# DeltaNet and MLP-mixer: exchanged chunks for odd head pairs in two of four batch elements

## The chip, the cores and the metric

The kernel runs on one core of a Trainium2 chip. The metric is the device time of one execution in microseconds (us); lower is better. Engines are named as in the profile: PE is TensorE (PEld its weight loads), DVE is VectorE, ACT is ScalarE, POOL is GpSimd, SP is SyncE, which issues all loads and stores here.

## The reference

Two blocks follow each other. The first is a DeltaNet recurrence, for 4 batch elements, 8 heads, 768 tokens and a head dimension of 48; the second a mixer over tokens and channels on rows of 8 x 48 = 384.

```python
k_n = k / (np.linalg.norm(k, axis=-1, keepdims=True) + 1e-06)
for t in range(S):
    y[:, :, t] = einsum('bhd,bhde->bhe', q[:, :, t], state)
    v_old = einsum('bhde,bhd->bhe', state, kt)
    state = state + bt * einsum('bhd,bhe->bhde', kt, vt - v_old)
x = y as (B, S, H * D)
h = np.maximum(x^T @ w_tok1, 0) @ w_tok2      # over tokens, 768 -> 256 -> 768
u = x + h^T
out = u + np.maximum(u @ w_ch1, 0) @ w_ch2    # over channels, 384 -> 1536 -> 384
```

All data are float32, and so are the matmuls.

## The kernel before

**The recurrence in chunks.** The tokens of an element are cut into 12 chunks of 64 (C); two chunks make a unit of 128 tokens (U). There are 24 units u (6 for each element, `b, c = divmod(u, NCH)`) and 48 steps t, one for each chunk of 64 tokens with all 8 heads. Heads stand in 4 pairs p, with a parity i in each. A unit is prepared apart from the state: `prep(u)` (from line 430) takes norms of the keys, turns keys and queries so that features lie along partitions (`kqts`), and makes the masked products p_g (L501, masked in L507); `invert` (L637, L642) and `join` (L715 to L734) invert the triangular matrices. `load_kq` and `load_v` fetch keys, queries and values from DRAM; `stacked` (lines 397 to 404) loads keys (kst) or values (v_st) with four DMA issues, so that of each head pair one head's chunk lies in partitions 0 to 63 and the other's in 64 to 127. Which one depends on the chunk alone: rows `PAR[i ^ cc]`, with cc the chunk in the unit.

**A step**, `recur(t)` (lines 740 to 811), then does the part that needs the state, s0, which lies with its 48 features on partitions 0 to 47 (parity 0) and 64 to 111 (parity 1):

- p_k = keys times state (L757, 8 products), then rest = p_k - v_st on DVE (L762);
- p_y = queries times state (L775) and p_w = inverse times rest (L779), interleaved; w_t is p_w copied by ACT (L783);
- p_s = keys times w_t (L791) and a second sum into p_y (L792), interleaved; the new state s1 = s0 - p_s on DVE (L801);
- two copies of p_y into the rows xb of the element, on ACT (L806).

The first chunk of an element has no p_k and no L775, and the last one no p_s. Each `yield` in it ends a part. A product of 64 rows by 64 columns uses one of the four 64x64 quarters of the PE array; its rows follow from the partitions of its operands and its columns from the partitions of its output. An fp32 product shows as two matmul records. p_k goes from rows of parity i to partitions `PAR[i ^ cc]`: for one step these are two of the four quarters. p_y and p_w together use all four, and so do p_s and the second p_y.

**PSUM** has eight banks: two for prep, three for the mixer, two that p_k, p_y, p_w and p_s take in turn (`ps_seq`), and one for warm-up matmuls (`p_warm`).

**The mixer**, `mixer(b)` (from line 943), takes an element when its 12 steps are written: over tokens (L950, L963), then over channels. Element 0 multiplies plainly (L1030); elements 1 to 3 use 15 combined weight blocks (`wide_fast`, p_r, L922, added up by DVE in L934 and ACT in L931 and L938), whose operands DVE forms in L891. The product with w_ch2 is p_o (L1052), added in L981.

**What sets the order.** Nothing is scheduled by the compiler: `tc.manual_schedule()` keeps every engine's instructions in the order in which they are recorded. All work is in generators, called jobs: k, p, h, f, j, v for a unit's loads and preparation, i for inversions, r for steps, m for mixers, w for weight pieces. A string written out by hand (`order`) tells which job goes on next, each time to its next `yield`; `r24*2 m1` records two parts of step 24 and one of mixer 1. The first half of the string is latency bound (loads and rounding of weights, the first units), the second mixes steps with mixer work.

Of the kernel before, what the change touches and what calls it, by code (L numbers as in the profile page):

```python
# [23 lines left out]
def kernel(  # L24
# [72 lines left out]

    def ps_seq(shape, name):
        return psum.tile(shape, FP32, name=name, tag="seq", bufs=2)
# [119 lines left out]
    p_warm = psum.tile([128, 4, 128], FP32, name="p_warm", tag="warm", bufs=1)  # L219

    def keep_warm(m):

        zero = warm[:, 0:128]
        while True:
            nc.tensor.matmul(
                p_warm[:, 0:m], zero, zero[:, None, :].to_broadcast([128, m, 128])
            )
            yield

    def warm_tiles():  # L230

        while True:
            for j in range(2):
                for r in PAR:
                    nc.tensor.matmul(p_warm[r, j], warm[r, 0:C], warm[r, 0:128])
            yield

    def load_beta():


        rows = mlp_pool.tile([B * H, S], FP32, name="b_rows", tag="xb")
        nc.sync.dma_start(out=rows, in_=beta.rearrange("b h s -> (b h) s"))
        yield
        p_b = ps_prep([128, NQ, B * NP], "p_b")
        for c in range(NQ):
            for par in range(2):
                nc.tensor.matmul(
                    p_b[PAR[par ^ c % 2], c], rows[:, c * C : (c + 1) * C],
                    ident[: B * H, par : B * H : 2],
                )  # L250
# [146 lines left out]
    def stacked(dst, src, u):  # L397
        rows = heads_of(src, u)
        for par in range(2):
            for cc in range(2):  # L400
                nc.sync.dma_start(
                    out=dst[PAR[par ^ cc], :, cc], in_=rows[par, cc]
                )
                yield
# [25 lines left out]
    def prep(u):  # L430
# [6 lines left out]
        bet = beta_st[:, b, :, 2 * c : 2 * c + 2]  # L437
# [15 lines left out]
        nc.vector.tensor_tensor(  # L453
            out=cs, in0=ksum.rearrange("s (p c) -> s p c", c=2), in1=bet, op=ALU.mult
        )
# [41 lines left out]
        for p in range(NP):  # L497
            for cc in range(2):
                for i in range(2):
                    f = PAR[i] if u < TU else FEATS[i]  # L500
                    nc.tensor.matmul(  # L501
                        p_g[cc][PAR[i ^ cc], p], kqt[f, p, cc, 0], kqt[f, p, cc]
                    )
        yield
        for cc in range(2):
            assert cc == 0 or before_in(u) is None or before_in(u) in walked
# [233 lines left out]
    def recur(t):  # L740
# [10 lines left out]
        heads = [(p, i, PAR[i ^ cc], PAR[1 - i]) for p in range(NP) for i in range(2)]  # L751

        if c > 0:
            p_k = ps_seq([128, NP, D], "p_k")
            for p, i, r, _ in heads:
                f = FEATS[i]
                nc.tensor.matmul(p_k[r, p], kqt[f, p, cc, 0], s0[f, p])  # L757
# [4 lines left out]
            nc.vector.tensor_tensor(  # L762
                out=rest, in0=p_k, in1=vsts[u][:, :, cc], op=ALU.subtract
            )
            yield
        else:
            rest = vsts[u][:, :, cc]

        assert u in scaled and u in joined
        p_y = ps_seq([128, NP, D], "p_y")  # L770
        p_w = ps_seq([128, NP, D], "p_w")
        for p, i, r, o in heads:
            if c > 0:
                f = FEATS[i]
                nc.tensor.matmul(  # L775
                    p_y[o, p], kqt[f, p, cc, 1], s0[f, p],
                    start=(p == 0), stop=False,
                )
            nc.tensor.matmul(p_w[r, p], gm[r, 2 * p + cc, TC], rest[r, p])  # L779
# [7 lines left out]
        if on:  # L787
            p_s = ps_seq([128, NP, D], "p_s")
        for p, i, r, o in heads:
            if on:  # L790
                nc.tensor.matmul(p_s[PAR[i], p], gm[r, 2 * p + cc, 0:C], w_t[r, p])  # L791
            nc.tensor.matmul(  # L792
                p_y[o, p], gm[r, 2 * p + cc, GC], w_t[r, p],
                start=(c == 0 and p == 0), stop=(p == NP - 1),
            )
        if cc == 1:
            walked.add(u)
        yield
        if on:
            if c > 0:  # L800
                nc.vector.tensor_tensor(out=s1, in0=s0, in1=p_s, op=ALU.subtract)  # L801
            else:
                nc.vector.tensor_copy(out=s1, in_=p_s)
            yield
        for i in range(2):
            nc.scalar.mul(  # L806
                y[:, :, D * i : D * i + D], p_y[PAR[1 - i]], 1.0 if c else -1.0
            )
# [340 lines left out]
    r12 s m0 v7 r12 w25 r12 w23 p10*3 f9 r12 j8 r13 w23 p12 w23 j8 m0 p11 r13*3 p11*2  # L1149
    w23 x w32 f9 v8 w30 w20 r13*2 k13 w32 w20 p10 r13 p11*3 w20 k13 r14*2 p12 k13 w32  # L1150
    p12 k13*3 m0*2 k13 w30 m0 k13 p11 w30*2 v8 k13 r14 k13*2 r14 p12*2 p11 k13 p12 p13
    r14 p12*3 m0 p12 p13 r14*2 m0 p13 w23 w25 p13 w33 v8*2 m0 j9 r15 p13 m0 w23 p13 r15
    w25 m0 p11 m0 r15 p13 r15 w33 m0*2 r15 p13*2 k14 w33 r15 k14 p13*2 w33 r16 m0 r15
    v8 k14*4 p12 w33 p11 r16 w27 w33 w31 m0 w27 w33 w29 w31*2 p13*2 j9 m0 p13*2 m0 j9
    k14 r16 j9 r16*3 k14 p14*2 r16 m0 r17*2 p14*3 m0*2 r17 i3 r17 i3*4 v10 m0 v10 r17*3
    i3*3 k15 m0 i3*2 v9 r18 i3*2 p14 m0 v10 k14 m0 i3 v9 i3 k15*4 v9 k15*3 m0*2 k14
    i3*9 k14 i3 k14 i3 p14 v9*2 m0*3 k15 r18 k15 p14 i3*6 m0*2 i3 v10 j9 k15 m0*4 k15
    m0*9 r18 p14*2 f11 r18*4 f10*2 p15*2 f12 v10 f12 f11 m0*2 p15*2 f10*2 f13 m0 r19
    p15 f12 f11 m0 f11 m0 r19 p14 f13 j10 f13 m0*2 r19 p15 j10 j11 r19*2 k16*8 m0*2 r19
    j10 j11 v11*3 r20 m0*2 r20 r19 j12 j11 r20 p15 k16 r20 m0 r20*2 p16*2 p15*3 k16 v11  # L1160
    p16*2 r21 r20 r21 m0 p15 r21 p16 r21 j12 p14 j12 k16*2 p14*2 k17*2 r21*3 m0 s k17*5
    p16*2 r22 v11 m0 r22*3 p16 m0 k17*4 r22 s v12 s j13 s p16 r22 k17 p16 r22 r23 p16*3
    v12 r23 v12 p15*4 p17*3 p14 p17 m0 p17 r23 m0 p17*2 r23 m0*2 p16 r23 p17*3 v12 p16
    m0 p17*4 m0 s m0 s*3 p17 m0 f12 m0 j13 s*4 r23 m0*3 v12 m0 i4*5 m0 i4*2 k18*8 m0 i4
    j13 r24 m0 i4 m0*2 r24 f13 r24 k18 m0 i4*2 k18 i4 m0*2 p18 i4 k18 p18*2 m0*2 i4 r24
    i4*3 m0 i4*2 k18 p18 r25 p18 m1 v14 r24 v14*3 i4 r25 m1*2 i4 k19 i4 k19*2 m1*3 r25
    k19 i4*2 v13 j13 r25 i4 p18 r25*2 i4 k19*4 m1 i4*2 m1 r25 v13*2 i4*2 v13 i4 j13 i4
    p19 r26 m1*2 p18 k19*4 m1 v13 r26 p19 m1*5 p18 f14 r26 f14 r26 p18 r26 f15 m1 r26
    m1*3 r26 m1*2 p19 f14 r27*2 f14 m1 r27 f15 p19 f15*2 p19 k20*5 p18 j14 m1*2 p18 p19
    r27*2 j14 j15 m1*2 j14 r27 m1 r27 k20*2 s j15 r28 p18 j15 p19 v14 k20*4 r28 m1*3  # L1170
    k20 m1 v15*2 s*2 p19 v15*2 r28*2 p19 r28 v15 m1 f16*3 r28 r29 p19 p20*2 r28 r29
    p20*2 p19 p20 k21*4 m1*3 p19 k21*4 r29*2 p20 p18*2 p20 m1*3 f17*2 m1*3 r29*3 j16
    m1*2 f17 m1 k21*4 m1*5 r30 j16 m1 r30 p20 m1 p19 m1 p18 m1 j16 p21 r30 p21 p20
    p19*2 p20 r30*3 p20 p21 p20 r31 p20*2 p21 r30 m1 r31*2 v16 r31 v16 m1 p21 f16 k22
    p21*2 r31 p21*2 r31*2 p20 r32 m1 p21*3 m1*2 p21*3 v16*2 i5 m1*2 k22*11 m1*7 v16 j17
    r32 m1*2 j17 f17 i5*2 m1*3 j17 i5 r32 i5*2 p22 r32 v17*2 i5*2 v17 m1*3 i5 m1*2
    r32*2 m1*3 i5*2 r33 r32 v17 r33 j17 v20 m1 i5 v20 i5 r33 p22*2 m1*4 i5 p22*4 m1*10
    r33 j17 v17 m1*3 i5 m1*2 k23*8 m1*3 r33 p22 r33 m1*7 r34*2 p23 m1*7 r33 i5 m1*2 r34
    p22 r34 p22 r34*2 m1 v20 i5*2 m1 r34 i5*2 m1 k23 m1 i5*3 m1*4 k23 r35 p22*2 m1*2
    p22*2 m1 i5*2 k23 m1 p23 m1*4 i5 m1 i5 m1 i5 p23 k23 r35 m1 i5*3 m1*8 v18 v20 i5  # L1180
    f21 p23 v18 f18*2 f19 m1 v18 p23*2 r35*2 m1*5 f18*2 p23*2 m1*3 v18 m1*4 p23 f21
    r35*2 f19 m1*2 f20 p23*4 v20 j18 m1 f19 m1*3 j18 m1*3 j18 j19*2 p23 j19 m1*2 p23
    f21 p22 f21 i6*2 v18 f20*2 r36*2 i6*3 f20 m1 r36 m1 r36 m1 r37*2 i6 m2*5 r36 r37*2
    m2 i6*6 r37 j20 i6*2 v19*2 r37 i6 f19 i6 j20 j21 r38 m2 v19*3 r38 j20 m2 r37 i6 r38
    i6*3 j21 r38*3 m2 r38 m2*2 i6 m2 r39*2 i6 m2*6 v21 r39 m2 r39 m2*2 r39 m2*2 r39
    m2*2 r39 j21 v21*2 m2 r40 m2*2 i6 r40*3 i6 j21 i6 j21 i6*2 r40*3 m2*3 r41 m2 r41 i6
    v21 i6 m2 r41 i6*3 f22*3 f23 m2 r41 v22 m2*6 r41*2 m2*4 v21 m2*5 r41 m2 r42*2 j22
    v22*3 m2*5 f23 r42 j22 f23 j23 r42*2 m2*2 r42*2 m2*7 r43 m2*5 r43*2 m2*3 f22 m2*2
    v23 m2*2 j22 m2*11 r43 m2*3 r43*3 j23*2 r44 m2*3 v23 v22 r44*3 m2*9 r44*3 f23 m2*2
    r45 j23 r45*2 m2 r45 m2*8 r45 m2*14 v23*2 m2*4 r45 r46 j23 m2*5 v23 m2 r46 m2 r45  # L1190
    m2*6 r46*2 m2 r46*2 m2*2 r46 r47 m2*2 r47*2 m2*4 r47 m2*7 r47*2 m3*6 m2*2 m3*6 m2*7
    m3 m2 m3*7 m2 m3 m2*3 m3*153
# [37 lines left out]
```

## Time and profile before

| | |
|---|---|
| median of 3 runs | 651.85 us (644.68, 651.85, 652.03) |
| the profiled execution | 649.33 us, its span 647.5 us |
| PE busy | 609.4 us, 94% of the span |
| PE weight loads busy | 529.7 us, 82% |
| DVE busy | 445.6 us, 69% |
| ACT busy | 258.1 us, 40% |
| POOL busy | 107.9 us, 17% |
| DMA issues | 510, all on SP |

How to read it: a group line names the kernel's line, the engine, the operation and its tiles, its shape and count, then its busy time and the mean duration of one in ns, then the engine's idle time just before and what ended it. A row of the timeline has the start, the length, the engine, the line and how many instructions were merged. Matmuls overlap, so a record lasts longer than the time it takes from the stream. Steps t = 24 to 35 (element 2) lie between about 268 and 400 us of the span, and t = 36 to 47 (element 3) between 411 and 530.

### The profile page before, as it was taken

The page shows a single profiled execution, that of the slowest core. Times are in us where ns is not written, and L with a number is a line of the kernel's source. Part 1 is how long each engine was busy: PE and PEld are TensorE (multiplying, and loading weights), DVE is VectorE, ACT ScalarE, POOL GpSimd, SP SyncE. Part 2 cuts the span into 40 slices and gives each one's busy share as a digit, 9 for nine tenths or more (in the row PEclk, how much of TensorE's full clock was granted, in tenths as well). Part 3 has the DMA queues.
Part 4 walks back from the last instruction along what each step waited for, and adds up shares of the span by engine and source line. Part 5 has one row for each costly group of instructions (what it writes and reads, how often), then busy time and mean ns, then how long its engine had stood idle before and what let it go on. Part 6 is the DMA issues. An engine that isn't in the chain of part 4 may idle for free.

```text
span 647.5 us, 22172 instructions
## 1 busy us (share of the span) xinstructions
PE 609.4 (94%) x9486; PEld 529.7 (82%) x9486; DVE 445.6 (69%) x1127; ACT 258.1 (40%) x623; POOL 107.9 (17%) x145
## 2 busy tenths in 40 slices
PE   7568887799999999999999999999999999999997
PEld 5346776567889988967989999869999987999997
DVE  4885664988789848888887989577826353372643
ACT  7748566446541242223633423125324240232240
POOL 1436335234320121002210102000000000000000
PEclk9859778699999999999999999999999999999999
DMA  9847446575643344434445113301110100000000
GB/s 189 176 100 171 105 120 150 115 195 119 138 103 79 88 103 92 97 77 108 96 79 130 45 49 70 75 4 30 28 35 3 31 3 0 25 1 25 1 26 24
DMA packets 135778, 50.30 MB, mean 78 GB/s; under 512 B 114656, under 2 KB 130144, under 8 KB 135680
## 3 DMA queue, kind: packets, MB, share of 16 engines
q1 hardware_dynamic: 135680, 48.89, 33.5%
q8 instruction: 74, 1.21, 0.8%
q14 instruction: 24, 0.20, 0.1%
HBM read 39.42 MB, written 9.44 MB: 75 GB/s over the span
## 4 chain that ended last, share of the span: by engine, by line
PE 83%; DVE 6%; DMA 3%; ACT 2%; issue 2%; SPq 2%; POOL 1%; DVEq 0%; POOLq 0%; ACTq 0%
PE p_o L1052 26%; PE p_r L922 20%; PE p_c L1030 7%; PE p_h L963 5%; PE p L950 5%; PE p_k L757 3%; PE p_y L775 3%; PE p_g L501 3%; PE p_s L791 3%; PE p_z L715 1%; PE p_w L779 1%; DVE sub L637 1%; PE p_y L792 1%; DVE x L642 1%; PE p_ut L973 1%
## 5 line engine op out<-in xcount | busy, mean ns | idle before, releaser
L1052 PE MATMUL p_o<-wc,r 128*128 128x192 f32 x720 | 127.8, 330 | 0.6 <-ACT u_t L977 0.6
L1052 PEld LDWEIGHTS p_o<-wc,r 128*128 128x128 f32 x720 | 116.6, 190 | 3.0 <-ACT u_t L977 1.1
L934 DVE TENSOR_TENSOR r<-r,p_r 128x512 f32<-128x512 f32 x90 | 59.8, 684 | 44.3 <-PE p_r L922 43.3
L981 DVE TENSOR_TENSOR xb<-xb,p_o 128x192 f32<-128x192 f32 x84 | 29.4, 350 | 62.1 <-PE p_o L1052 61.9
L931 ACT COPY r<-p_r 128x512 f32<-128x512 f32 x54 | 31.6, 586 | 99.7 <-PE p_r L922 86.1
L642 DVE TENSOR_TENSOR x<-x,sub 128x84 f32<-128x84 f32 (+24 forms) x178 | 59.2, 333 | 6.1
L637 DVE TENSOR_TENSOR sub<-x 128x84 f32<-128x84 f32 (+24 forms) x178 | 57.4, 322 | 6.3 <-DMA x<-n_dram 2.4
L1030 PE MATMUL p_c<-u_t,wc 128*128 128x256 f32 x216 | 50.8, 386 | 0.6 <-ACT u_t L977 0.6
L414 POOL TENSOR_TENSOR v_st<-v_st,nrm 128x384 f32<-128x384 f32 x24 | 20.7, 865 | 183.2 <-DMA v_st<-in_v_dram 128.5
L1052 PE MATMUL p_o<-wc,s 128*128 128x192 f32 x288 | 50.8, 330 | 0.3 <-DVE xb L981 0.3
L1052 PEld LDWEIGHTS p_o<-wc,s 128*128 128x128 f32 x288 | 46.8, 190 | 1.2 <-DVE xb L981 0.6
L1030 PEld LDWEIGHTS p_c<-u_t,wc 128*128 128x128 f32 x216 | 39.8, 190 | 6.5 <-ACT u_t L977 0.9
L938 ACT ACTIVATE r<-r 128x512 f32<-128x512 f32 x54 | 33.9, 631 | 24.4 <-DVE r L934 24.0
L806 ACT ACTIVATE xb<-p_y 64x192 f32<-64x192 f32 x96 | 31.2, 325 | 24.4 <-PE p_y L792 7.6
L473 POOL TENSOR_TENSOR mb<-mask_c,cs 128x512 f32<-128x512 f32 x20 | 21.0, 1049 | 118.1 <-DVE cs L453 80.3
L922 PE MATMUL p_r<-u_t,wc 128*128 128x128 f32 x288 | 38.5, 277 | 0.0
L783 ACT COPY w_t<-p_w 128x192 f32<-128x192 f32 x48 | 15.3, 318 | 56.9 <-PE p_w L779 56.4
L922 PE MATMUL p_r<-t_d,wc 128*128 128x128 f32 x288 | 37.3, 280 | 0.0
L950 PE MATMUL p<-xb,w 128*128 128x384 f32 x96 | 36.5, 532 | 0.2 <-ACT xb L806 0.2
L922 PEld LDWEIGHTS p_r<-u_t,wc 128*128 128x128 f32 x288 | 35.3, 192 | 0.3
L922 PEld LDWEIGHTS p_r<-t_d,wc 128*128 128x128 f32 x288 | 34.0, 191 | 0.9
L757 PE MATMUL p_k<-s_t,kq 48*64 48x48 f32 x656 | 28.4, 228 | 5.0 <-DVE s_t L801 5.0
(171 smaller groups left out, 1191.7 us busy)
## 6 DMA issues: line engine op xcount, KB each, us to landing
d<-in_moe_w_ch_dram SPq DMA_DIRECT2D x24, 384.0 KB, 4.1
v_st<-in_v_dram SPq DMA_DIRECT2D x96, 48.0 KB, 2.7
out_dram<-xb SPq DMA_DIRECT2D x23, 192.0 KB, 1.9
kst<-in_k_dram SPq DMA_DIRECT2D x64, 48.0 KB, 2.7
n_dram<-gm SPq DMA_DIRECT2D x72, 32.0 KB, 1.9
pads<-in_k_dram SPq DMA_DIRECT2D x24, 96.0 KB, 2.5
pads<-in_q_dram SPq DMA_DIRECT2D x24, 96.0 KB, 2.6
gm<-w_dram SPq DMA_DIRECT2D x72, 32.0 KB, 2.0
```

Of the source, the lines that this page charges most:

```text
L637: nc.vector.tensor_tensor(out=tmp, in0=y[:, :, 0:s, s : s + 1].to_broadcast([n, k, s, w]), in1=y[:, :, s : s + 1, s + 1 : m].to_broadcast( ...
L642: nc.vector.tensor_tensor(out=y[:, :, 0:s, s + 1 : m], in0=y[:, :, 0:s, s + 1 : m], in1=tmp, op=ALU.add,)
L757: nc.tensor.matmul(p_k[r, p], kqt[f, p, cc, 0], s0[f, p])
L806: nc.scalar.mul(y[:, :, D * i : D * i + D], p_y[PAR[1 - i]], 1.0 if c else -1.0)
L922: nc.tensor.matmul(p[:, i], pieces[i // width][:, at : at + 128], f[f"u{n}"], start=first and i == 0, stop=True, skip_group_check=True,)
L931: nc.scalar.copy(o, p)
L934: nc.vector.tensor_tensor(out=o, in0=o, in1=p, op=ALU.add if sign > 0 else ALU.subtract)
L938: nc.scalar.activation(o, o, ACTF.Relu)
L950: nc.tensor.matmul(p_1[dh], piece_of(w1, c, 0)[:, dh * 128 : (dh + 1) * 128], xb[:, c], start=(c == 0), stop=(c == NCH - 1),)
L963: nc.tensor.matmul(p_h, piece_of(w2, j, c * 128)[:, c * 128 : (c + 1) * 128], r1[j], start=(j == 0), stop=(j == NDH - 1),)
L1030: nc.tensor.matmul(p_c[:, k], piece_of(wc1, cb, f * 128)[:, f * 128 : (f + 1) * 128], u_t[:, cb], start=(cb == 0), stop=(cb == NCB - 1),)
L1052: nc.tensor.matmul(p, a[:, m], wc2[:, m, j], start=(start and i == 0), stop=(i == NM - 1), skip_group_check=True,)
```

## The change

For units 12 to 23 (elements 2 and 3, steps 24 to 47) the chunks of odd head pairs are exchanged: in `stacked`, in beta (through a selection matrix `pick` made by four POOL copies), in cs, in the products p_g and in the steps. A step then uses rows `PAR[i ^ cc ^ (p & 1)]`, so that the p_k of even pairs lie on two quarters and those of odd pairs on the other two. Loads of keys and values for these units have eight DMA issues with half the heads each in place of four. rest, the new state and the copies of y are made for even and odd pairs apart: two, two and four instructions in place of one, one and two. Three PSUM banks become tiles of their own for the whole kernel (`q_a`, `q_b`, `q_c`, in place of `ps_seq` and `p_warm`), and p_k, p_s, p_y and p_w have fixed columns in them. The order string is the same up to step 12 and new from there to the end; one warm-up part less is in it.

```diff
-    def ps_seq(shape, name):
-        return psum.tile(shape, FP32, name=name, tag="seq", bufs=2)
...
-    p_warm = psum.tile([128, 4, 128], FP32, name="p_warm", tag="warm", bufs=1)
+    SW = 12
+    seq = [psum.tile([128, 512], FP32, name=f"q_{n}", bufs=1) for n in "abc"]
+    p_warm = seq[2].rearrange("s (m n) -> s m n", m=4)
+
+    def swaps(u):
+        return int(u >= SW)
+
+    def slot_of(u, p, cc):
+        return cc ^ (p & swaps(u))
...
+    def in_bank(at, col, n):
+        return seq[at][:, col : col + n * D].rearrange("s (x d) -> s x d", d=D)
...
     def stacked(dst, src, u):
         rows = heads_of(src, u)
+        if swaps(u):
+            b, c = divmod(u, NCH)
+            chunks = src[b].rearrange("(x h par) t d -> par h t x d", h=2, par=2)
+            for par in range(2):
+                for e in range(2):
+                    for h in range(2):
+                        at = c * U + (e ^ h) * C
+                        nc.sync.dma_start(
+                            out=dst[PAR[par ^ e], h::2, e],
+                            in_=chunks[par, h, at : at + C],
+                        )
+                    yield
+            return
...
+        p_w = in_bank(2 if sw else 0, 4 * D, NP)
+        if sw:
+            p_k = in_bank(0, 0, 2), in_bank(2, 0, 2)
+            p_s = in_bank(0, 2 * D, 2), in_bank(1, 2 * D, 2)
+            p_y = in_bank(1, 4 * D, 2), in_bank(0, 4 * D, 2)
+        else:
+            p_k = p_s = (in_bank(0, 0, NP),)
+            p_y = (in_bank(1, 0, NP),)
...
-                nc.tensor.matmul(p_k[r, p], kqt[f, p, cc, 0], s0[f, p])
+                nc.tensor.matmul(part(p_k, r, p), kqt[f, p, cc, 0], s0[f, p])
...
-            nc.vector.tensor_tensor(
-                out=rest, in0=p_k, in1=vsts[u][:, :, cc], op=ALU.subtract
-            )
+            v_st = vsts[u]
+            for h in range(sw + 1):
+                nc.vector.tensor_tensor(
+                    out=rest[:, h :: sw + 1], in0=p_k[h],
+                    in1=v_st[:, h :: sw + 1, first[h]], op=ALU.subtract,
+                )
...
+            for h in range(sw + 1):
+                o, x = s1[:, h :: sw + 1], s0[:, h :: sw + 1]
+                if c > 0:
+                    nc.vector.tensor_tensor(out=o, in0=x, in1=p_s[h], op=ALU.subtract)
+                else:
+                    nc.vector.tensor_copy(out=o, in_=p_s[h])
+            yield
+        for h in range(sw, -1, -1):
+            for i in range(2):
+                nc.scalar.mul(
+                    y[:, h :: sw + 1, D * i : D * i + D], p_y[h][PAR[1 - i]],
+                    1.0 if c else -1.0,
+                )
```

More of the change, by code (lines that the diff above doesn't have):

```diff
@@ L224, in keep_warm @@
         while True:
+            assert len(steps) <= 2 * SW
             nc.tensor.matmul(
@@ L232, in warm_tiles @@
         while True:
+            assert len(steps) <= 2 * SW
             for j in range(2):
@@ L750, in recur, with part @@
         s0, s1 = s_t[t % 2], s_t[(t + 1) % 2]
-        heads = [(p, i, PAR[i ^ cc], PAR[1 - i]) for p in range(NP) for i in range(2)]
+        sw = swaps(u)
+        first = [slot_of(u, p, cc) for p in range(NP)]
+        heads = [
+            (p, i, PAR[i ^ first[p]], PAR[1 - i]) for p in range(NP) for i in range(2)
+        ]
+        p_w = in_bank(2 if sw else 0, 4 * D, NP)
[6 more added lines that the diff above has]
+            p_y = (in_bank(1, 0, NP),)
+        def part(x, r, p):
+            return x[p % 2][r, p // 2] if sw else x[0][r, p]
         if c > 0:
-            p_k = ps_seq([128, NP, D], "p_k")
             for p, i, r, _ in heads:
                 f = FEATS[i]
-                nc.tensor.matmul(p_k[r, p], kqt[f, p, cc, 0], s0[f, p])
+                nc.tensor.matmul(part(p_k, r, p), kqt[f, p, cc, 0], s0[f, p])
             keyed.add(t)
@@ L761, in recur, with w_product @@
             rest = rest_t
-            nc.vector.tensor_tensor(
-                out=rest, in0=p_k, in1=vsts[u][:, :, cc], op=ALU.subtract
-            )
+            v_st = vsts[u]
+            for h in range(sw + 1):
+                nc.vector.tensor_tensor(
+                    out=rest[:, h :: sw + 1], in0=p_k[h],
+                    in1=v_st[:, h :: sw + 1, first[h]], op=ALU.subtract,
+                )
             yield
-        else:
-            rest = vsts[u][:, :, cc]
         assert u in scaled and u in joined
-        p_y = ps_seq([128, NP, D], "p_y")
-        p_w = ps_seq([128, NP, D], "p_w")
         for p, i, r, o in heads:
+            def w_product():
+                x = rest[r, p] if c > 0 else vsts[u][r, p, first[p]]
+                nc.tensor.matmul(p_w[r, p], gm[r, 2 * p + first[p], TC], x)
+            early = sw and (p, i) == (0, 0)
+            if early:
+                w_product()
             if c > 0:
@@ L775, in recur @@
                 nc.tensor.matmul(
-                    p_y[o, p], kqt[f, p, cc, 1], s0[f, p],
-                    start=(p == 0), stop=False,
-                )
-            nc.tensor.matmul(p_w[r, p], gm[r, 2 * p + cc, TC], rest[r, p])
+                    part(p_y, o, p), kqt[f, p, cc, 1], s0[f, p],
+                    start=(p <= sw), stop=False, skip_group_check=True,
+                )
+            if not early:
+                w_product()
         if cc == 1:
@@ L786, in recur, with s_product @@
         on = c < NQ - 1
-        if on:
-            p_s = ps_seq([128, NP, D], "p_s")
         for p, i, r, o in heads:
-            if on:
-                nc.tensor.matmul(p_s[PAR[i], p], gm[r, 2 * p + cc, 0:C], w_t[r, p])
+            g = 2 * p + first[p]
+            def s_product():
+                nc.tensor.matmul(
+                    part(p_s, FEATS[i] if sw else PAR[i], p),
+                    gm[r, g, KC if sw else slice(0, C)], w_t[r, p],
+                    start=(c == 0 and p == 0) if sw else True, stop=True, skip_group_check=True,
+                )
+            if on and not sw:
+                s_product()
             nc.tensor.matmul(
-                p_y[o, p], gm[r, 2 * p + cc, GC], w_t[r, p],
-                start=(c == 0 and p == 0), stop=(p == NP - 1),
-            )
+                part(p_y, o, p), gm[r, g, GC], w_t[r, p],
+                start=(c == 0 and p == 0), stop=True, skip_group_check=True,
+            )
+            if on and sw:
+                s_product()
         if cc == 1:
@@ L799, in recur @@
         if on:
[L800 to L803, printed above, removed]
-            yield
[L805 to L808, printed above, removed]
+            for h in range(sw + 1):
+                o, x = s1[:, h :: sw + 1], s0[:, h :: sw + 1]
+                if c > 0:
+                    nc.vector.tensor_tensor(out=o, in0=x, in1=p_s[h], op=ALU.subtract)
+                else:
+                    nc.vector.tensor_copy(out=o, in_=p_s[h])
+            yield
+        for h in range(sw, -1, -1):
[3 more added lines that the diff above has]
+                    1.0 if c else -1.0,
+                )
         written.add(t)
@@ L1154 @@
[L1154 to L1159, printed above, removed]
```

113 lines of the change are left out of this document (70 added, 43 removed).

## The prediction

> **What bounds the kernel now.** I read the windows of busy time first, then the chain that ended last, then the timeline of single steps. The windows (busy time in us by engine, with counts) show where a change can pay:
>
> ```profile
> core 0: us, PE busy (x) PEld busy (x) DVE busy (x) ACT busy (x) POOL busy (x), PEclk, DMA share, GB/s
> 0.00:100.00 100.00, 76.01 (x1994) 58.78 (x1994) 66.42 (x180) 67.24 (x177) 40.48 (x60) 0.82 0.69 142
> ...
> 300.00:400.00 100.00, 99.14 (x1683) 93.96 (x1676) 86.88 (x213) 42.50 (x99) 14.84 (x21) 1.00 0.36 80
> 400.00:500.00 100.00, 100.00 (x1632) 87.16 (x1632) 64.88 (x173) 34.95 (x82) 4.98 (x8) 1.00 0.14 30
> ```
>
> From 200 us on TensorE has work all the time, at the full granted clock (1.00); only before that is there room. The chain says the same, and that the recurrence is a small part of it:
>
> ```profile
> PE 83%; DVE 6%; DMA 3%; ACT 2%; issue 2%; SPq 2%; POOL 1%; DVEq 0%; POOLq 0%; ACTq 0%
> PE p_o L1052 26%; PE p_r L922 20%; PE p_c L1030 7%; PE p_h L963 5%; PE p L950 5%; PE p_k L757 3%; PE p_y L775 3%; PE p_g L501 3%; PE p_s L791 3%; PE p_z L715 1%; PE p_w L779 1%; DVE sub L637 1%; PE p_y L792 1%; DVE x L642 1%; PE p_ut L973 1%
> ```
>
> A busy TensorE can hide small gaps, since a matmul's record outlasts its turn. So I compared starts of successive records with the steady distance of their kind (0.112 us for 128 moving columns, 0.163 for 192). From 180 us to the end only three places lose over 0.25 us to a dependency inside the recurrence (about 1.4 us together), and the last element's mixer about 1.3 us more. Hence from step 12 on, where the order changes, time falls mainly when TensorE's own work falls.
>
> One step (t = 39; columns: start, length, engine, line, operation):
>
> ```profile
> 436.78 0.67 PE L757 MATMUL p_k<-s_t,kq 48*64 48x48 f32 x16
> ...
> 437.50 0.36 DVE L762 TENSOR_TENSOR rest<-p_k,v_st 128x192 f32<-128x192 f32 x1
> ...
> 438.18 0.25 PE L775 MATMUL p_y<-s_t,kq 48*64 48x48 f32 x1
> 438.19 0.13 PEld L779 LDWEIGHTS p_w<-rest,gm 64*64 64x64 f32 x1
> ...
> 438.65 0.22 PE L779 MATMUL p_w<-rest,gm 64*64 64x48 f32 x1
> 438.79 0.97 PEld L922 LDWEIGHTS p_r<-u_t,wc 128*128 128x128 f32 x8
> ```
>
> Eight fp32 products are 16 records. The 16 of p_k, which use two of the array's four 64x64 quarters, go from first to last start in 0.67 - 0.22 = 0.45 us. The 32 of p_y and p_w, on four quarters, take 438.65 - 438.18 = 0.47. So each quarter takes one record per 0.06 us, and p_k is the only product of the step that leaves two quarters empty.
>
> **The change, part by part.**
>
> *Keys times state on four quarters.* 22 steps (t = 24 to 47 without the two first chunks) have a p_k. Sixteen records on four quarters are half of what the 32 do in 0.47: 0.23. Saving 0.22 each, 22 x 0.22 = 4.8 us, all on TensorE and so on the path. Bounds: 0, if these products do not overlap; 22 x (0.45 - 0.20) = 5.5. I take 4.8, since p_y has the same operands' shapes and banks split in the same way. The p_s/p_y and p_y/p_w groups fill four quarters before and after: 0.
>
> *The new order on TensorE.* In the built program, runs of full-array work fall from 114 to 110 and one 128-column warm-up product goes. Entering a small-tile group costs 0.205 instead of 0.112 us from the last p_r start, leaving it 0.148 instead of 0.06: 0.18 a visit. 4 x 0.18 + 0.22 = 0.9 us less (bounds 0 to 0.9).
>
> *Longer hand-overs.* rest (L762) and the state update (L801) become two VectorE instructions of 96 columns. From 0.353 at 192 and 0.28 at 128 (L891) 96 columns are about 0.25: 0.50 in place of 0.35. The copy of y (L806, ACT, 0.325 for 64x192) becomes four of 64x96; from 0.257 at 16x128 and 0.365 at 32x256 about 0.24 each. Now the even y and the odd state share a bank, and the built program waits accordingly: a y copy waits for the state update of its bank, and the next p_k for the two y copies of bank a where these stand ahead of it. In the old trace the y copy runs beside the update (300.25 against 300.21). From the end of p_s to the next p_k I get 0.05 + 0.25 + 0.06 + 2 x 0.24 + 0.05 = 0.9 us, against 0.45. It costs only where TensorE has nothing in between. I added up the matmuls between the groups in the built order: 16 of 22 hand-overs have 1.9 us or more; five have 0.8 to 1.1, which is just enough, or the y copies stand behind p_k there; one (t = 30) has nothing. That one is a gap already today:
>
> ```profile
> 327.89 0.69 DVE L507 TENSOR_TENSOR gm<-p_g,mb 128x512 f32<-128x512 f32 x1 [0.20 <-PE p_g L501]
> ...
> 328.36 0.66 ACT L806 ACTIVATE xb<-p_y 64x192 f32<-64x192 f32 x2
> 328.50 0.34 DVE L801 TENSOR_TENSOR s_t<-s_t,p_s 128x192 f32<-128x192 f32 x1
> ...
> 328.90 0.67 PE L757 MATMUL p_k<-s_t,kq 48*64 48x48 f32 x16 [0.66 <-DVE s_t L801]
> ```
>
> It grows by 0.45. At t = 28 p_s now follows p_w with nothing between, a copy w_t of 0.32 with its signals: 0.45. Two short covers of today (t = 31) become long: -0.3. With 0.2 for the five tight ones: +0.8 (bounds -0.3 and 22 x 0.45 = 10).
>
> *VectorE.* 22 x 0.15 for rest, 22 x 0.15 for the state, 12 second halves of cs at 0.17 (L453), 2.0: 8.6 us more. Its cover is TensorE's time. In 260 to 400 us, where steps 24 to 35 lie, the 20 us windows sum to 121.3 busy of 140. There it gets 12 x 0.30 + 7 x 0.17 = 4.8 more, while TensorE's time shrinks by 3: about 11 us of slack remain of 19. I take 1 us (bounds 0 and 11, all of the slack being needed as it is). Some 47 more waits of about 0.05 us are in that bound.
>
> *ScalarE.* 24 x (4 x 0.24 - 2 x 0.325) = 7.4 us on an engine that is 40% busy: nothing, beyond the hand-over above. *GpSimd* makes the selection matrix in four copies before the beta product; it idles from 2.4 to 5.5 us, and beta lands at 5.2: nothing.
>
> *Loads.* 24 loads of keys and values take eight issues in place of four, half as large.
>
> ```profile
> 357.51 1.77 SPq L357 DMA_DIRECT2D pads<-in_k_dram  x4
> 359.38 2.58 SPq L401 DMA_DIRECT2D kst<-in_k_dram  x4
> ```
>
> An issue of a 48 KB load is 0.65 of SP. For the half-size one the nearest row, with as many pieces, is pads at 0.44; the shortest, w_dram, 0.35. So two cost 0.7 to 0.9, and the 96 split loads 5 to 24 us more of SP's time. The queue is in order: behind it stand the other pads loads, the n_dram and w_dram pieces and the stores. SP issued 95 us in 250 to 400 and 23 of 25 in 325 to 350, so it is full in one place. Loads run ahead of use by several us (a whole unit's buffer), so I take 0 (bounds 0 and 5).
>
> Sum: -4.8 - 0.9 + 0.8 + 1.0 = -3.9. The profiled execution took 649.33 (span 647.5): 645.4. The shown runs lie on both sides of it, median 651.85 (2.5 above), lowest 644.68 (4.7 below), so I let it stand and say 645.5.
>
> **A rule against the change.** VectorE needs 0.35 us for one p_k today against TensorE's 0.67. The Trainium skill, TensorEngine Tiling (Array Packing), PSUM Bottleneck, says that packing speeds up the matmuls and not the emptying of PSUM, which may become the bottleneck. The trace agrees as far as it goes: p_k falls towards 0.45 with its tail while rest rises to 0.50. By that rule the first rival below would come true, with its 655.4.
>
> **Rivals.**
> 1. *VectorE becomes the bound in steps 24 to 35* (slower than before). For: 19.27 of 20 us busy in 360 to 380, and the new order packs more of it into steps 30 to 31 and 34 to 35. Against: 13% of the stretch is free today, and only 5 us come in. It decides once the useless slack exceeds 11 us of 137. Price: the whole 11 in place of 1: 649.33 - 4.9 + 11 = 655.4.
> 2. *p_k does not gain*, because the four quarters do not overlap with 48-row operands, or because the first p_k waits for ACT more often than I counted: 649.33 - 0.9 + 0.8 + 1 = 650.2. Against: p_y, same shape, shares the array well.
> 3. *SP runs late* in steps 28 to 35, and transposes and p_g wait as at 240 us today, where a pads load stands in the chain. 5 us: 650.4; several such places together exceed 2%.
> 4. *Better than the sum*: hand-overs and VectorE all covered, 649.33 - 6.4 = 643, 638.5 against the lowest run.
>
> **How the numbers follow.** Forecast 0.55 (its own range 641 to 650), VectorE 0.17, no gain 0.10, SP 0.10, better 0.08. The range to 8 in 10 is 639 to 656: better-than-sum at the lowest run, and VectorE as the bound. 2% of 651.85, about what a measurement here can tell, is 13 us: 638.8 to 664.9. No case but a piece of the best one and a repeated SP or VectorE delay leaves it: faster 0.04, same 0.89, slower 0.07.
>
> **What would show it.** Right: p_k from t = 24 on as x16 of about 0.45 us in place of 0.67; TensorE still without gaps after 200 us; y copies starting after the state update. Wrong: p_k still 0.67 (rival 2); VectorE over 95% in 260 to 400 with p_r waiting for it (rival 1); loads of pads or v_st as releasers of TensorE (rival 3). The forecast fails if any change before step 12, where the order is the same, moves the time.

## The result, and the profile after

The changed kernel takes 665.5 us (median of 4 runs, 664.52 to 666.74), the kernel before beside it 651.18: a ratio of 1.0275 with a 95% interval of 1.0227 to 1.0322. The ratios here compare fast runs with fast runs alone, so this one is not the quotient of the two medians (1.022). The kernel is slower by 14 us by the medians and by 18 us by the ratio, where 645.5 us was forecast, and lies outside the range of 639 to 656. The profiled execution took 664.79 us, its span 663.0.

The chain of work that ended last, from the page of the changed kernel (share of the span by engine, then by line):

```profile
PE 53%; SPq 12%; DVE 11%; DMA 9%; issue 8%; ACT 5%; POOL 2%; DVEq 0%; POOLq 0%; ACTq 0%
PE p_o L1136 18%; PE p_r L1006 16%; SPq L431 7%; PE p L1034 4%; DVE sub L686 2%; DMA d<-in_moe_w_ch_dram 2%; DVE x L691 2%; PE p_h L1047 2%; SPq L633 2%; PE q_a L820 2%; PE q_c L838 1%; DMA v_st<-in_v_dram 1%; PE p_g L550 1%; SPq L382 1%; PE q_b L870 1%
```

TensorE's share of the chain fell from 83% to 53%, and SP's queue stands second with 12%, from 2%. L431 is the split load. The windows of busy time show where TensorE has gaps now:

```profile
200.00:300.00 100.00, 95.71 (x1334) 81.62 (x1333) 73.55 (x193) 27.24 (x74) 10.65 (x15) 0.98 0.35 81
300.00:400.00 100.00, 92.70 (x1610) 83.63 (x1609) 79.63 (x224) 38.60 (x107) 13.99 (x20) 0.98 0.35 78
```

Between 200 and 400 us TensorE is busy for 11 us less than it was, at a granted clock of 0.98 in place of 1.00. VectorE (the third number after the window's length) is less busy there too, 79.63 against 86.88 in 300 to 400: it is not the bound.

What the change was for did come. In the timeline of step 39 the first and the last row of p_k (two records each) are:

```profile
453.72 0.26 PE L820 MATMUL q_a<-s_t,kq 48*64 48x48 f32 x2
...
453.94 0.23 PE L820 MATMUL q_c<-s_t,kq 48*64 48x48 f32 x2
```

From 453.72 to 454.17 are 0.45 us for the 16 records, against 0.67 before, and rest begins 0.58 us after p_k, not 0.72. So the steps are shorter and the kernel longer. The time is lost where the order differs and the split loads run: p_k of step 13 starts at 155.4 us (158.5 before), that of step 47 at 536.8 (522.7 before). The loads tell why. By source line, the issues of the kernel before (shortest, median and longest in ns) are

```profile
L401 SPq DMA_DIRECT2D kst<-in_k_dram x64: 596/615/1722, 13.0 to 361.3; - x64
```

and the half-size ones of the changed kernel

```profile
L431 SPq DMA_DIRECT2D kst<-in_k_dram x96: 595/606/1645, 127.2 to 390.5; - x96
```

Half the bytes cost SP the same 0.61 us. With the 0.04 us between two issues, 192 x 0.65 in place of 96 x 0.65 makes 62 us more of SP's time. Of the 192 issues 100 start between 225 and 375 us, where SP now issues 21.6 to 23.1 us in every 25; before, it was 7.5 to 22.7. A queue that is full falls behind. The chain in order of time (start, length, what) ahead of element 2's first p_w (inverse times v, as the first chunk has no rest):

```profile
279.71 0.60 SPq L431
280.31 0.04 issue
280.36 0.61 SPq L431
280.96 0.04 issue
281.01 1.99 DMA v_st<-in_v_dram
283.07 0.09 issue
283.16 0.84 POOL v_st L452
284.04 0.74 PE q_c L838 x16
```

One issue after another, back to 270.34, then the landing, GpSimd's scaling of v, and only then the product. TensorE stood still for 2.8 us. It pays a second time, as the windows around it show (the granted clock is the third number from the end):

```profile
281.00:284.00 3.00, 0.23 (x2) 0.00 (x0) 1.16 (x3) 0.00 (x0) 0.84 (x2) 1.00 0.23 40
284.00:288.00 4.00, 3.96 (x53) 2.47 (x54) 2.12 (x8) 0.83 (x3) 0.14 (x1) 0.69 0.40 106
288.00:292.00 4.00, 4.00 (x29) 2.93 (x29) 3.34 (x10) 0.00 (x0) 0.00 (x0) 0.88 0.42 117
```

After the gap the clock is 0.69 and 0.88 for some microseconds in which TensorE is busy the whole time. The same happens after the gap that ends at 335.94 us (2.6 us; pieces of the inverse, w_dram, were late in the same queue). Three more gaps of 1.2 to 1.5 us, worked out from successive starts, end at 184.82, 361.47 and 368.62.

### The profile page after: what moved, and what is told of

It reads as the page before. It is cut to its first block, busy times and chain, and to the rows that moved or that the text cites. A ratio compares the mean times of both kernels' runs of the same rounds, so it can differ in the third digit from the quotient of the medians.

```text
span 663.0 us, 22462 instructions
## 1 busy us (share of the span) xinstructions
PE 612.6 (92%) x9484; PEld 530.0 (80%) x9484; DVE 447.1 (67%) x1183; ACT 264.5 (40%) x671; POOL 105.6 (16%) x149
## 4 chain that ended last, share of the span: by engine, by line
PE 53%; SPq 12%; DVE 11%; DMA 9%; issue 8%; ACT 5%; POOL 2%; DVEq 0%; POOLq 0%; ACTq 0%
PE p_o L1136 18%; PE p_r L1006 16%; SPq L431 7%; PE p L1034 4%; DVE sub L686 2%; DMA d<-in_moe_w_ch_dram 2%; DVE x L691 2%; PE p_h L1047 2%; SPq L633 2%; PE q_a L820 2%; PE q_c L838 1%; DMA v_st<-in_v_dram 1%; PE p_g L550 1%; SPq L382 1%; PE q_b L870 1%
## 5 line engine op out<-in xcount | busy, mean ns | idle before, releaser
L1136 PEld LDWEIGHTS p_o<-wc,r 128*128 128x128 f32 x720 | 118.8, 193 | 3.0 <-ACT u_t L1061 1.1
L1136 PE MATMUL p_o<-wc,s 128*128 128x192 f32 x288 | 52.7, 339 | 0.3 <-DVE xb L1065 0.3
L1136 PEld LDWEIGHTS p_o<-wc,s 128*128 128x128 f32 x288 | 49.1, 198 | 1.3 <-DVE xb L1065 0.6
L1047 PE MATMUL p_h<-r,w 128*128 128x384 f32 x96 | 32.5, 491 | 0.0
L309 POOL TENSOR_TENSOR wc<-w_f,d 128x384 uint32<-128x384 uint32 x24 | 24.6, 1028 | 49.1 <-ACT d L303 13.0
L889 ACT ACTIVATE xb<-q_b 64x192 f32<-64x192 f32 (+1 forms) x96 | 27.3, 284 | 10.7 <-PE q_b L870 9.3
```

The lines of the kernel that those rows point to most:

```text
L1047: nc.tensor.matmul(p_h, piece_of(w2, j, c * 128)[:, c * 128 : (c + 1) * 128], r1[j], start=(j == 0), stop=(j == NDH - 1),)
L1136: nc.tensor.matmul(p, a[:, m], wc2[:, m, j], start=(start and i == 0), stop=(i == NM - 1), skip_group_check=True,)
```

## The experiments

Theory 1: SP's in-order queue is full, because a half-size issue costs as much as a whole one; the loads come late, and that is nearly all of the loss. Rivals: the new order (theory 2); shared banks and halved instructions (theory 3). Ratios are to the kernel before on the same chip, with 95% intervals; differences in us between runs are worked out from the ratios.

**Whole loads, four runs around two questions.** The first kernel takes the split out of the loads of the changed one. It leaves out the exchange of odd pairs with it, so its output is not the reference's; every instruction behind the loads stays, and its time alone is read:

```diff
-                    for h in range(2):
-                        at = c * U + (e ^ h) * C
-                        nc.sync.dma_start(
-                            out=dst[PAR[par ^ e], h::2, e],
-                            in_=chunks[par, h, at : at + C],
-                        )
+                    nc.sync.dma_start(
+                        out=dst[PAR[par ^ e], :, e], in_=rows[par, e]
+                    )
                     yield
```

> The changed kernel, but the keys and values of units 12 to 23 are loaded with four whole issues each, without the exchange of odd head pairs (everything after the loads is as in the changed kernel, so odd pairs of elements 2 and 3 are computed from the chunks that were not exchanged). Theory 1 (SP's queue is full: each half-size load issue costs 0.61 us as a whole one does, 96 more of them 60 us of SP): 642 to 649 us, gaps of TensorE back to about 1.4 us in each 50. Theory 2 (the new order puts loads and steps badly, whatever the number of issues): 660 or more. Theory 3 (the shared banks, halved instructions on VectorE and ScalarE): 660 or more.

Measured: 655.03 us, ratio 1.0082 (1.0044 to 1.0119). Against 1.0275 the split issues cost 1.9%, 12.5 us; but it is not back at the 642 to 649 of theory 1, so something else costs too.

The second puts the split, and nothing else, into the kernel before:

```diff
-                nc.sync.dma_start(
-                    out=dst[PAR[par ^ cc], :, cc], in_=rows[par, cc]
-                )
+                for h in range(2 if u >= 12 else 1):
+                    n = 2 if u >= 12 else 1
+                    nc.sync.dma_start(
+                        out=dst[PAR[par ^ cc], h::n, cc], in_=rows[par, cc][:, h::n]
+                    )
```

> The kernel before, with nothing changed but that the keys and values of units 12 to 23 are loaded with eight issues of half the heads each in place of four. Theory 1: slower by much of what the change lost, 660 to 670 us, SP back to back from about 225 to 390. Theories 2 and 3: 649 to 653, no change, since neither the order nor the steps are touched.

Measured: 689.35 us, 1.0546 (1.0472 to 1.0619). Theory 1 holds and its price was set too low: in the old order the split costs 36 us, about twice what the whole change lost. The first line of its chain, from its page:

```profile
PE 55%; SPq 8%; DVE 6%; DMA 5%; ACT 2%; issue 2%; POOL 0%; POOLq 0%; ACTq 0%; DVEq 0%
```

One window of 10 us shows gaps and a low clock together, 6.90 us busy at 0.66:

```profile
320.00:330.00 10.00, 6.90 (x130) 6.54 (x133) 4.94 (x19) 1.96 (x6) 1.61 (x2) 0.66 0.49 121
```

The third and the fourth kernel are the changed one with the order string of before, with split and with whole loads.

> The changed kernel with the order string of before; the eight issues, the exchange, the banks and the halved instructions stay. Theory 1: 658 to 668, the loads are late in either order. Theory 2: 645 to 650, as the order was the fault. Theory 3: 660 or more.

Measured: 689.75 us, 1.056 (1.0473 to 1.0647), far above the 658 to 668 of theory 1. Theory 3 gave 660 or more here too; the next run tells them apart.

> The changed kernel with the order string of before and the four whole load issues (no exchange in the loads of units 12 to 23, everything after them as in the changed kernel, so odd pairs of elements 2 and 3 are computed from the chunks that were not exchanged). Theory 1 and theory 2: 644 to 650, and the difference to the run with whole loads and the new order is the price of the order alone, under 3 us. Theory 3: 660 or more.

Measured: 650.74 us, 0.999 (0.996 to 1.002). So theory 3 is out as the main cause, and the new order was not the fault: with split loads it takes some 19 us off (1.056 to 1.0275). With whole loads it costs 0.9% (0.999 to 1.0082), 6 us where under 3 were expected. And the whole change without the split comes out level with before, though TensorE's busy time fell from 609.4 to 604.2 us. The waits of TensorE between 200 and 540 us in this kernel (engine, line, waited for: us, times, longest) say where the gain went:

```profile
PE q_a L817 <- ACT xb L886: 2.2, 4, 1.1
PE q_b L867 <- ACT w_t L851: 1.1, 1, 1.1
PE q_c L835 <- DVE rest L824: 0.9, 2, 0.5
```

The first row is p_k waiting for the copies of y out of the bank that it shares with them; before, the only wait of p_k there was 0.7 us for the state.

**Other queues and other forms.** In two kernels the second of each two half-size issues leaves SP: `(nc.gpsimd if h else nc.sync).dma_start(...)`, and the same with `nc.scalar`.

> The changed kernel, but of each two half-size load issues the second (odd pairs) goes out on GpSimd's queue in place of SP's; the whole computation stays. Theory 1 (SP's time for 96 more issues is what is lost against the 655.0 us of whole loads in the same order): about 655 us (652 to 659), if an issue on GpSimd, 16% busy, costs it under 1 us. Rival (the loads come late because there are more and smaller transfers, not because of SP): stays at 663 to 668.

Measured: 655.59 us, 1.0041 (0.9997 to 1.0084). All 192 small transfers are still there, and the loss of the split is gone. This kernel computes everything, the exchange included. By source line, GpSimd and SP pay the same for an issue:

```profile
L431 SPq DMA_DIRECT2D kst<-in_k_dram x48: 601/607/2018, 127.9 to 369.4; - x48
L431 POOL DMA_DIRECT2D kst<-in_k_dram x48: 585/592/753, 133.8 to 370.2; - x48
```

and its chain has SP at 1%:

```profile
PE 79%; DVE 8%; ACT 5%; issue 3%; DMA 3%; SPq 1%; DVEq 0%; ACTq 0%
```

The Trainium skill, DMA: Bandwidth & Descriptors, Issuing engines are not separate DMA queues, says that starting transfers from several engines saves only the sequencer's time, usually small beside the transfer. The runs agree that this time is what is saved; here it was not small, as 0.61 us of issue stand beside a median of 2.1 us to landing, in a queue that the next issue waits for.

> The changed kernel, but of each two half-size load issues the second goes out on ScalarE's queue. Theory 1: SP is free as in the run before it, but ScalarE, which makes w_t and y in every step, takes 96 issues of some 0.6 us between them: 655 to 662 us, with TensorE waiting for w_t in a few places. Rival (transfers, not issues): 663 to 668 or more.

Measured: 686.06 us, 1.054 (1.0469 to 1.061). That is far above what theory 1 gave, and the transfers are not the reason either, since the same ones on GpSimd's queue cost nothing that can be told. On ScalarE an issue costs the same (median 0.617 to 0.620) but stands in front of w_t, whose waiters are TensorE's:

```profile
PE q_b L870 <- ACT w_t L854: 4.2, 2, 3.7
```

The longest wait ahead of such an issue on ScalarE, for a semaphore, took 3.78 us, and what stands behind it waits too: w_t stood behind these issues in three places, for 8.7 us together. That ScalarE was 40% busy said nothing about room for them.

Two kernels ask what an issue's time goes by. The first loads slot 0 pair by pair over 128 partitions: `out=dst[:, p, 0]`, `in_=heads2[p, :, at : at + C]`.

> The changed kernel, but in slot 0 of each unit from 12 on the loads go by head pair over all 128 partitions (four issues of 128 rows of 48 numbers, 24 KB each) in place of four of 64 rows of two heads; slot 1 as in the changed kernel. The same count of issues and the same bytes; the whole computation stays. If SP's time for an issue goes by its form (128-partition issues of x and w_dram took 0.34, 64-partition ones 0.61 whatever their size): 0.34 to 0.45 for these, 48 x 0.2 to 0.25 = 10 to 13 us less of SP's time and, by theory 1, 660 to 664 us. If it goes by the count of rows or pieces (128 in both): 0.61 and 664 to 667 us.

Measured: 663.11 us, 1.0173 (1.0108 to 1.0239). The source line:

```profile
L432 SPq DMA_DIRECT2D kst<-in_k_dram x48: 507/557/1412, 131.5 to 386.4; - x48
```

0.55 us: better than 0.61 and far from the 0.34 that I took from the contiguous 128-partition issues; partitions alone do not set it. The saving is 96 x 0.06 = 6 us of SP, and the time is inside the range given for the success, but the mechanism is only half there, and the interval overlaps that of the changed kernel. The other kernel is the one before with the split by tokens, 32 partitions and all four heads (`out=dst[r, :, cc]`, r half of the rows).

> The kernel before with the loads of keys and values of units 12 to 23 in eight issues, as in the run that split by heads (689.4 us), but each with 32 partitions and four heads in place of 64 partitions and two heads: the same count and the same 24 KB. If an issue's time goes by its partitions: 0.43 to 0.45 us each (as pads and n_dram, 32 partitions), 27 us more of SP in place of 58, and 660 to 672 us. If it goes by the issue alone: 0.61 and 686 to 692. If by size: the same time for both forms, 0.61, since the size is the same.

Measured: 659.83 us, 1.0137 (1.0075 to 1.02), and

```profile
L405 SPq DMA_DIRECT2D kst<-in_k_dram x112: 311/430/1852, 13.0 to 373.8; - x112
```

Same count, same 24 KB, 0.43 in place of 0.61 us (16 of the 112 are whole loads of earlier units). So the time of an issue follows its form, not its size. SP has 28 us more to do than before (192 x 0.475 - 96 x 0.655, gaps between issues included) in place of 62, and the loss is 9 us in place of 36. The loss grows faster than SP's time. That some of that time fits into the queue's slack for nothing, and the rest comes back with a lower clock, is how I read it; no run shows it by itself.

**Where the gain of the four quarters went.** The first kernel is the old order with whole loads, with p_k back on two quarters: `part(p_k, PAR[i ^ cc] if sw else r, p)`. Its output is not the reference's either.

> As the run with the old order and whole loads (650.7 us), but the 8 products p_k of a step write the partitions by chunk alone, so that they use two quarters of the array again; loads are not exchanged and the rows of p_k of odd pairs are not the ones that rest expects, so it is this timing alone that is read. If keys times state on four quarters is worth what it measures on TensorE: p_k back at 0.67 and 4.8 us slower than that run, about 655.5 us. If the gain is lost in waits: 650 to 652.

Measured: 654.97 us, 1.0058 (1.0019 to 1.0097) against 0.999 (0.996 to 1.002) with four: 0.7%, or 4.4 us, with intervals that just touch. The trace bears it out: p_k is back at 0.45 us from first to last start, from 0.23. So the gain on TensorE is there, about as large as forecast. The same run also prices what takes it back: it holds the halved instructions and the shared banks, but neither the gain, nor the split, nor the new order, and takes 3.8 us more than the kernel before (1.2 to 6.3).

Then the halved instructions alone, in the kernel before (rest and the state in two, y in four; `for h in range(n)` over `[:, h::n]`, n = 2 from unit 12 on):

> The kernel before, with rest and the new state made in two VectorE instructions of 96 columns and y in four ScalarE copies of 64 by 96 from step 24 on; banks, loads, quarters and order as before, the whole computation stays. If the halved instructions are what gives the 4.4 us back: 653 to 656. If it is the shared banks: 650 to 652.

Measured: 652.5 us, 1.0037 (0.9999 to 1.0076), about 2.4 us, between the two expectations, with an interval that reaches down to 0. And the shared bank alone, in the old order with whole loads: odd copies of y with another source (`w_t[PAR[1 - i], 1::2] if h else p_y[h][PAR[1 - i]]`).

> As the run with the old order and whole loads (650.7 us), but the y copies of odd pairs read the tile w_t in place of PSUM bank a, with the same shape and count (so the output of odd pairs in elements 2 and 3 is not y). If p_k waiting for the y copies of the shared bank is the dear hand-over: 2 to 3 us less, 647.5 to 649, and the waits of p_k for xb (2.2 us) gone. If the halved instructions on VectorE and ScalarE are: no change.

Measured: 649.7 us, 0.9959 (0.991 to 1.0007) against 0.999: 2 us in the expected direction, but the intervals overlap, so the time shows nothing. In its trace p_k no longer waits for y. The two sizes together would make up the 4.4 us; neither is told from 0.

Next, versions that might beat both kernels. The old order with half of the split issues on GpSimd:

> The changed kernel with the order of before and the second of each two half-size issues on GpSimd's queue; the whole computation stays. Theory 1 (only SP's issue time made the split loads dear): about the 650.7 us of the old order with whole loads, 649 to 653, and 39 us below the 689.8 us of the same kernel with all issues on SP. If the split loads are dear by themselves: 670 or more.

Measured: 651.49 us, 0.9988 (0.9941 to 1.0035). It takes 37 us off the run that differs in the queue alone (1.056), with the whole computation in both. So the split is dear by SP's time for the issues, and not by its transfers, in either order. Then ten moves in the order string, such as

```diff
-r27 k20*2 s j15 r28 p18
+r27 k20*2 s j15 m1 r28 p18
...
-v22 m2*6 r41*2 m2*4 v21 m2*5 r41 m2 r42*2
+v22 m2*6 r41*3 m2*4 v21 m2*6 r42*2
...
-r44*3 f23 m2*2 r45 j23 r45*2 m2 r45
+r44*3 f23 m2*4 r45 j23 r45*3
```

> As the run before it, with ten small moves in the order string at the places where TensorE waits for a hand-over in the run with whole loads and old order (before steps 28, 31, 44 and 45 a part of the mixer is pulled ahead of p_k; the y copies of step 41 stand directly behind the state update, so that they are ahead of the mixer's ReLU on ScalarE; those of step 37 one part earlier; w_t of step 32 ahead of the squares that wait for a key load). If the gain of four quarters (4.4 us) was given back in hand-overs at these places: 3 to 5 us below that run, 645 to 648. If it was given back elsewhere, VectorE's or ScalarE's busy time: no change.

Measured: 655.23 us, 1.008 (1.0044 to 1.0115), slower than the run before it. The waits at steps 28, 42 and 44 closed, and the move at step 45 opened a larger one. The timeline there:

```profile
495.08 0.68 DVE L1088 TENSOR_TENSOR s<-r 128x512 f32<-128x512 f32 x1
...
498.21 0.25 DVE L827 TENSOR_TENSOR rest<-q_a,v_st 128x96 f32<-128x96 f32 x1
...
498.68 0.34 PE L838 MATMUL q_c<-rest,gm 64*64 64x48 f32 x1 [2.86 <-DVE rest L827]
```

The mixer part that I pulled ahead of p_k brought its six VectorE instructions with it, 3.3 us, and rest stands behind them. I had counted only what it issues on TensorE. After that gap the clock fell to half:

```profile
499.00:504.00 5.00, 5.00 (x46) 4.82 (x39) 0.04 (x1) 0.32 (x1) 0.00 (x0) 0.50 0.01 3
```

The next kernel keeps only the moves that closed a gap (steps 28, 32, 41 and 44), and leaves the keys of unit 12 on SP.

> The changed kernel with the order of before, the second half-size issues of v, and of k from unit 13 on, on GpSimd's queue (those of k of unit 12 stay on SP, since GpSimd reached them late in the run with all of them, and p_k of step 15 waited 1.3 us for it), and only those moves in the order that closed a gap: the mixer parts before p_k of steps 28 and 44, the y copies of step 41 directly behind its state update, w_t of step 32 ahead of the squares. The whole computation stays. If the gain of four quarters went into such hand-overs: 2 to 4 us below 651.5, 647 to 649.5, and below the kernel before by 0.2 to 0.6%. If not: 651 to 653.

Measured: 652.1 us, 1.0021 (0.9978 to 1.0064): no gain that can be told. Against the run with all of the second issues on GpSimd, TensorE's idle time between 450 and 500 us fell from 1.7 to 0.3 us. Between 150 and 200 it rose from 1.3 to 2.6, with p_k of step 15 still waiting 1.4 us for the state: moving unit 12's keys did not help. From 332 to 340 the granted clock was 0.79 where it had been 1.00. Last, one VectorE instruction over two banks of a common tile, in place of two:

> As the run with the covered hand-overs, but the three banks are one tile, and rest and the new state are each made by one VectorE instruction of 192 columns that reads two banks, in place of two of 96. The whole computation stays. If the halved VectorE instructions cost 2.4 us, as in the kernel before with halves: 1 to 3 us below that run (645 to 648). If the waits of shared banks are all that is left: the same within 1 us. A single tile may also make more waits than three: then slower.

Measured: 666.8 us, 1.0286 (1.0234 to 1.0338). The common tile brings back waits that three tiles had parted; its first row of waits, between 150 and 560 us:

```profile
PE q_all L821 <- ACT xb L901: 7.6, 10, 1.7
```

p_k waits ten times for copies of y, where the kernel with three tiles waits 0.3 us in all. It does not tell the price of halving. No version here is faster than the kernel before by more than its interval.

## Why the prediction was wrong, point by point

**What bounds the kernel** was right for the kernel before, and it was the wrong question for this change. A full TensorE stays full only as long as its inputs come in time, and the tightest supplier, SP, was seen ("23 of 25 in 325 to 350") and not treated as a second bound.

**Loads: the step that failed.** It read: "So two cost 0.7 to 0.9, and the 96 split loads 5 to 24 us more of SP's time", "so I take 0 (bounds 0 and 5)". An issue of half the size was priced by pads at 0.44 us, since it has as many pieces, and by w_dram at 0.35. It takes 0.606. SP got 62 us more, and the split alone costs 12.5 us in the new order and 36 in the old one, where 0 was taken. The nearest row was the load itself, 0.61 with the same 64 partitions; a price by size was an assumption that no row bore out, since the rows of other sizes differed in form. The bound of 5 us was also taken from a single late place, while SP issued back to back from 270.34 to 280.96 us ahead of one gap and was as full in six stretches of 25 us.

**Keys times state: right.** 0.23 us from first to last start and 4.4 us in the total, for 0.23 and 4.8.

**The new order: wrong sign by itself.** Forecast -0.9; with whole loads it costs 0.9%. That it spares some 19 us with split loads was not seen, since I looked only for what it does on TensorE.

**Hand-overs and VectorE: too small.** Forecast +0.8 and +1. With whole loads in the old order TensorE worked 5.2 us less and the kernel was no faster; the waits of TensorE of 0.2 us and more between 200 and 540 us add up to 6.4 us there, 0.9 before. Without the gain of p_k the same kernel takes 3.8 us more than before, for the 1.8 forecast. Halving alone measured 2.4 us (interval 0 to 5), and p_k waited 2.2 us for y where it had waited for the state alone, 0.7 us. In the old order copies of y stand behind mixer activations of 0.63 us on ScalarE; I had counted the cover on TensorE and not what stands ahead of y on its own engine.

**Rivals.** The third, SP late, came true, at two and a half times its 5 us (12.5), and with v_st as the releaser that it named; its own sentence, that several such places exceed 2%, was the better forecast. The first, VectorE as the bound, is false: less busy than before. The rule on emptying PSUM, which would have given 655.4, did not decide: halving costs 2.4 us where SP costs 36 in the same order. The second, no gain of p_k, is false. In the fourth, 6.4 takes the upper bound of p_k, 5.5, where the sum has 4.8, and against the lowest run it gives 638.3 us, not 638.5; nothing hangs on it.

## What to carry to other kernels

Price a split transfer at the issue time of the form that it keeps, from the row of the same partitions, and add it to the queue in the window where that queue is already full; gaps of TensorE of 2.6 us and more cost 1.6 to 2 times their length here. An instruction that moves takes everything along that its part issues on every engine, so the queue to look at is that of the engine whose result the next step waits for. Where one issuing queue is full, another with room and nothing urgent behind it (GpSimd here) takes half of the split issues at almost no cost; one with urgent work behind it (ScalarE) does not.

## What the runs showed of the hardware that was not expected

**The clock after a gap.** Three gaps of 2.6 to 2.9 us are followed by a granted clock of 0.50, as windows of 1 us show: from about 285.5 to 288.9 and from 336.7 to 340.2 in the changed kernel, 3.4 us each, and from 497.6 to 504.4 in the run with ten moves, 6.8 us that begin within the gap. So such a gap costs 1.6 times to twice its length (in the changed kernel 2.8 us and 1.7 more, 4 x 0.31 + 4 x 0.12; in the other 2.9 and as much again). The Trainium skill, TensorE: Matmul & The Clock Gate, Part 1: The HAM clock gate, states half rate after an idle window of about 3.4 us and full rate after as much work. The traces agree on the half and, in two of the three places, on how long it lasts; they show it after gaps shorter than that.

**VectorE beside GpSimd.** In the new order with whole loads, GpSimd runs several instructions in a row beside the inversion's instructions on VectorE:

```profile
297.70 0.83 POOL L449 TENSOR_TENSOR v_st<-v_st,nrm 128x384 f32<-128x384 f32 x1 [20.54 <-PE p_h L1044]
297.75 0.91 DVE L688 TENSOR_TENSOR x<-x,sub 128x108 f32<-128x108 f32 x1
298.49 1.07 POOL L518 TENSOR_TENSOR mb<-mask_c,cs 128x512 f32<-128x512 f32 x1
298.69 0.97 DVE L683 TENSOR_TENSOR sub<-x 128x84 f32<-128x84 f32 x1
```

In the old order with whole loads the instruction of 84 columns takes 0.23 to 0.25 us in all eight places, and here 0.97 while GpSimd works and 0.24 to 0.25 in the other seven:

```profile
348.01 0.24 DVE L683 TENSOR_TENSOR sub<-x 128x84 f32<-128x84 f32 x1
```

Beside this row of the old order no GpSimd instruction runs. The Trainium skill, SBUF — State Buffer, SBUF: two separate sides, says that VectorE with two operands in SBUF and GpSimd hold one pair of ports in turn, each for a whole instruction; the rows agree, each VectorE instruction ending about when the GpSimd one beside it does. p_h waits 2.0 us for VectorE behind them, and the same wait, 2.9 us, is in the run with the new order and GpSimd's queue, where the 84 columns take 0.88 us beside GpSimd. That this is what the new order costs with whole loads is argued from the trace; it was not tried by itself.

**The price of an issue.** 64 partitions with rows of 192 bytes: 0.61 us for 48 KB as for 24 KB; 128 partitions with such rows: 0.55; 32 partitions: 0.43; on SP, ScalarE and GpSimd alike where it was tried (64 partitions). What sets it is left open.
